# Attention and gated-convolution layer, forward and backward, on one Trainium2 core: the rows of q and of the gradient laid out as four blocks and transposed by one transfer, dP taken out of PSUM by ScalarE, and new leads for the planned order

## The chip, the cores and the metric

The kernel runs on one core of one Trainium2 chip. The core has TensorE (PE; its weight loads are shown as PEld), VectorE (DVE), ScalarE (ACT), GpSimd (POOL) and SyncE (SP), which here does nothing but issue transfers. All engines share SBUF; TensorE writes to PSUM, from which DVE and ACT read. The transfers run on 16 DMA engines.

The metric is the device time in microseconds of one execution. The time before is the median of three runs.

## The reference

`B, T, D, K = 2, 4000, 144, 5`, all in bfloat16. The forward part, cut to what matters:

```
xa  = layernorm(x)
q, k, v = split(xa @ w_qkv)
p   = softmax(q @ k.T * D ** -0.5)
glob = (p @ v) @ w_att_out
u, g = split(gelu(xa @ w_mlp_in))
loc = (u * dwconv(layernorm(g), dw_csgu)) @ w_mlp_out
m   = concat(glob, loc)
out = x + (m + dwconv(m, dw_merge)) @ w_merge
```

The kernel returns `out` and, for a given `grad_out`, the gradients of x and of the seven weights (the `vjp` of this function).

## The kernel before, in words

The 4000 positions of a batch entry are cut into 32 tiles of 125 rows; 64 tiles in all. The attention phase (`phase_att`, L1182) walks them in steps `s`. Weights are multiplied together beforehand, so that scores are a product of a projected row block and the normalised input itself, and the gradient with respect to p, dP, is likewise a product of a projected gradient and that input.

For a tile `i` the following is done, spread over several steps:

- `jit_mm` (L1223): seven matmuls make `pj`, 125 rows x 288: the projected query (144) and the projected gradient (144). ScalarE copies it to `qb` (L1232). POOL copies the last 16 columns of both halves four times each into a second tile `qr` (`rems`, L1240), 32 columns apart, since the matmuls on these 16 columns use four different groups of 32 rows of TensorE.
- `jit_tr` (L1242): TensorE transposes `qb` and `qr` in four blocks of 128 columns (L1246) into a PSUM tile, and ScalarE copies that to `qt` (L1248). `qt` has three buffers.
- `quad` (L1254): in each of the four `products` of a step, two blocks of scores of tile `s` and two blocks of dP of tile `s-1`, 500 columns each, are made from `qt`: four matmuls over 128 rows (L1257) and four over 16 rows (L1264).
- `S_min` (L1279): DVE takes the scores out of PSUM into `Pbuf` with the running minimum; `P_exp` (L1285): ScalarE makes the exponential.
- `PdP` (L1291): dP times P goes to `Sbuf`. In three of the four products ScalarE copies dP out of PSUM (L1295) and DVE multiplies in SBUF (L1297); in the fourth (`q == 3`) DVE multiplies straight from PSUM (L1293).
- SP transposes `Pbuf` to `PT` (L1289) and `Sbuf` to `ST` (L1473), each in two halves of 16 blocks of 128 x 128, by the DMA. `PT` and `ST` have one buffer: a half may be written only after the matmuls on it of the tile before.
- `Y_half` (L1306) and `Z_half` (L1344): 16 matmuls on each half of PT and of ST, into `yz`. From Y come `yn`, which SP stores to Yn_d (L1320), and on POOL the scaled rows `QBs` (L1324 to L1328). From Z comes `zn`, which SP stores (L1349) and transposes to `zt` (L1356).
- `X_group` (L1391): for up to three blocks of 125 rows, matmuls on Sbuf and Pbuf of two tiles, and where they are due on `zt` and `dhT`, into a PSUM tile `X`, which DVE adds to `acc` (L1397).

Between these stand the units of the gated convolution (`local_units`, L577 to L745), which use TensorE, ACT, DVE and POOL, store `ug` and transpose `dhr` to `dhT` on SP's queue (L703); in the second part of the first batch entry the loading and preparation of the second one take their place (SP's loads into gq, xa_aug and others); and at the end the merge and the final weight gradients.

The order of the instructions on each engine from step 2 on is not the program's. The class `Planner` (L779) collects the instructions, groups matmuls, takes what depends on what, gives each group a cost, and lays them out as a list scheduler; each engine then runs its groups in that fixed order. A group's rank is its place in the program plus a lead from the table `LEAD` (L782), whose keys are kind by kind: phase (A or T), engine, tile, size, and for some tiles the turn within a step. A negative lead lets a kind be taken earlier, a positive one later. Steps 0 and 1 (`head`, with `jit_q` L1410 and `jit_b` L1424 for the first two tiles) keep the order of the program. In what depends on what, two readers of one PSUM bank are kept in order only when they are on the same engine (L1012).

Of the kernel before, what the change touches and what calls it, by code (L numbers as in the profile page):

```python
# [8 lines left out]
BF = mybir.dt.bfloat16  # L9
F32 = mybir.dt.float32  # L10
ACT = mybir.ActivationFunctionType
# [767 lines left out]
class Planner:  # L779


    LEAD = {  # L782
# [15 lines left out]
    }  # L798


# [114 lines left out]
    def plan(self, i0, i1, window=400, late=1 << 40):  # L915
# [38 lines left out]
        for ins in todo:  # L954
# [3 lines left out]
            for w, lst in ((False, ins.ins), (True, ins.outs)):  # L958
                for a in lst:
# [42 lines left out]
                    if w:  # L1002
                        for h, q in Rd:
                            if h != g and self.meet(q, bank):
                                preds[g].add(h)
                        full = lambda q: not psum and q[0] >= r[0] and q[1] <= r[1] and len(r[2]) == 1 and q[2][0][0] >= r[2][0][0] and q[2][-1][1] <= r[2][0][1]
                        W[:] = [z for z in W if not full(z[1])]
                        Rd[:] = [z for z in Rd if not full(z[1])]
                        W.append((g, r))
                    else:  # L1010
                        if psum:
                            after[g].update(h for h, _ in Rd if h != g and groups[h]["e"] == groups[g]["e"])  # L1012
                        Rd.append((g, r))
        lastpe = {}
        for g, G in enumerate(groups):
# [166 lines left out]
def phase_att(k, W, SS, A, head, E0, E1, prep, hooks):  # L1182
# [21 lines left out]
    PT = ab.tile([128, NB, 128], BF, name="PT")  # L1204
    ST = ab.tile([128, NB, 128], BF, name="ST")
    QBs = ab.tile([PB, NPB, 2, D], BF, name="QBs")
    qbr = [ab.tile([PB, 2, D], BF, name="qb%d" % i) for i in range(3)]
    qrr = [ab.tile([PB, 256], BF, name="qr%d" % i) for i in range(3)]
    znr = [ab.tile([128, 256], BF, name="zn%d" % i) for i in range(2)]

    def clr():
        for t_ in qrr:
            nc.gpsimd.memset(t_[:], 0.0)
        for t_ in znr:
            nc.gpsimd.memset(t_[:], 0.0)
# [7 lines left out]
    def jit_mm(i):  # L1223
        S, ti = bs(i)
        pj = ps_w.tile([PB, 2 * D], F32, tag="w")
        nc.tensor.matmul(pj[:], S.R[:, ti], W.RW[:, 0:2 * D], start=True, stop=False)
        nc.tensor.matmul(pj[:, 0:D], S.xaT_m[:, ti], W.Q0[:], start=False, stop=False)
        for kk in range(5):
            h = i % NB + 4 - kk
            nc.tensor.matmul(pj[:, D:2 * D], S.goT[:, h * PB:(h + 1) * PB], W.VUT[:, kk, 0:D], start=False, stop=(kk == 4))  # L1230
        qb = qbr[i % 3]
        nc.scalar.copy(qb[:], pj[:].rearrange("p (a b) -> p a b", b=D))  # L1232
        QB[i] = qb
        for h in range(2):
            rems(nc.gpsimd.tensor_copy, i, h)

    def rems(eng, i, h):
        v = qrr[i % 3][:].rearrange("p (a r c) -> p a r c", a=4, r=2)
        v = v[:, 0:4:3, :, 0:DR] if h == 0 else v[:, 1:3, :, 0:DR]
        eng(v, QB[i][:, h, 128:D].rearrange("p (a r c) -> p a r c", a=1, r=1).to_broadcast([PB, 2, 2, DR]))  # L1240

    def jit_tr(i):  # L1242
        qb = QB[i]
        pt = ps_w.tile([128, 4, 128], BF, tag="w")
        for q, src in enumerate((qb[:, 0, 0:128], qrr[i % 3][:, 0:128], qrr[i % 3][:, 128:256], qb[:, 1, 0:128])):
            nc.tensor.transpose(pt[:, q, 0:PB], src, W.ident[0:PB, 0:PB])  # L1246
        qt = gw.tile([128, 4, PB], BF, tag="qt")
        nc.scalar.copy(qt[:], pt[:, :, 0:PB])  # L1248
        QT[i] = qt

    def pchunk(pb, c2):
        return Pbuf[0:PB, pb, c2 * 1024:(c2 + 1) * 1024]
# [1 line left out]
    def quad(work, stacked=True):  # L1254
        pp = [ps_sg.tile([PB, 2, 512], F32, tag="sg", name="ps") for _ in range(len(work) // 2)]
        for r, (i, h, c) in enumerate(work):
            mm = nc.tensor.matmul(pp[r // 2][:, r % 2, 0:CH], QT[i][:, 3 * h, :], bs(i)[0].xaT_m[:, c * CH:(c + 1) * CH], start=True, stop=False)  # L1257
        with tc.issue_after(mm.ins):
            for r, (i, h, c) in enumerate(work):
                S = bs(i)[0]  # L1260
                q = c % 4 if stacked else 3
                rs = slice(32 * q, 32 * q + DR)
                xr = S.XR[rs, (c // 4) * CH:(c // 4 + 1) * CH] if stacked else S.R[rs, c * CH:(c + 1) * CH]
                nc.tensor.matmul(pp[r // 2][:, r % 2, 0:CH], QT[i][rs, 1 + (q // 2 + h) % 2, :], xr, start=False, stop=True)  # L1264
        return [p[:, :, 0:CH].rearrange("p h (a b) -> p h a b", b=PB) for p in pp]

    def S_work(i, c2):
# [142 lines left out]
    def jit_q(i):  # L1410
        S, ti = bs(i)
        pj = ps_w.tile([PB, 2 * D], F32, tag="w")
        nc.tensor.matmul(pj[:, 0:D], S.R[:, ti], W.RW[:, 0:D], start=True, stop=False)
        nc.tensor.matmul(pj[:, 0:D], S.xaT_m[:, ti], W.Q0[:], start=False, stop=True)
        QB[i] = qbr[i % 3]
        nc.scalar.copy(QB[i][:, 0, :], pj[:, 0:D])
        rems(nc.scalar.copy, i, 0)
        QT[i] = gw.tile([128, 4, PB], BF, tag="qt", name="qt")
        pt = ps_w.tile([128, 4, 128], BF, tag="w")
        for q, src in enumerate((QB[i][:, 0, 0:128], qrr[i % 3][:, 0:128], qrr[i % 3][:, 128:256])):  # L1420
            nc.tensor.transpose(pt[:, q, 0:PB], src, W.ident[0:PB, 0:PB])
        nc.scalar.copy(QT[i][:, 0:3, :], pt[:, 0:3, 0:PB])

    def jit_b(i):  # L1424
        S, ti = bs(i)
        pj = ps_w.tile([PB, 2 * D], F32, tag="w")
        nc.tensor.matmul(pj[:, D:2 * D], S.R[:, ti], W.RW[:, D:2 * D], start=True, stop=False)
        for kk in range(5):
            h = i + 4 - kk
            nc.tensor.matmul(pj[:, D:2 * D], S.goT[:, h * PB:(h + 1) * PB], W.VUT[:, kk, 0:D], start=False, stop=(kk == 4))  # L1430
        nc.scalar.copy(QB[i][:, 1, :], pj[:, D:2 * D])
        rems(nc.scalar.copy, i, 1)
        pt = ps_w.tile([128, 4, 128], BF, tag="w")
        for q, src in enumerate((qrr[i % 3][:, 0:128], qrr[i % 3][:, 128:256], QB[i][:, 1, 0:128])):
            nc.tensor.transpose(pt[:, q, 0:PB], src, W.ident[0:PB, 0:PB])
        nc.scalar.copy(QT[i][64:112, 1, :], pt[64:112, 0, 0:PB])
        nc.scalar.copy(QT[i][0:48, 2, :], pt[0:48, 1, 0:PB])
        nc.scalar.copy(QT[i][:, 3, :], pt[:, 2, 0:PB])

    steps = head(dict(pads=pads, clr=clr, jit_q=jit_q, jit_b=jit_b, jit=lambda i: (jit_mm(i), jit_tr(i))))  # L1440
    i0 = 0
# [2 lines left out]
    for s in range(NT + 1):  # L1444
# [30 lines left out]
        def products(q):  # L1475
# [5 lines left out]
            ps = quad(S_work(s, q) + (dP_work(s - 1, q ^ 1) if ok(s - 1) else []))  # L1481
            S_min(s, q, ps[0])
            if ok(s - 1):
                PdP(s - 1, q ^ 1, ps[1], q == 3)

        if s < 2:
            for q in range(8):
# [740 lines left out]
```

## Time and profile before

| | |
|---|---|
| median of 3 runs | 1297.62 us (1297.03 to 1298.73) |
| the profiled execution, its own time | 1296.92 us |
| its span, first to last instruction | 1295.1 us |
| granted TensorE clock, mean | 0.995 |
| matmuls | 15,874 |
| bytes moved by DMA | 185.78 MB, 143 GB/s over the span |

The span in 40 equal slices, where each digit is the busy share in tenths (9 is 90% or more), shows the same picture from some 60 us to 1150 us: TensorE at 9, DVE at 8 to 9, the DMA engines at 6 to 9. Before lies the head (loads, layer norm, products of weights), behind it the merge and the end.

In rows of instructions, "x62 | 35.9, 580 | 30.8 <-PE pt" reads: 62 instructions, 35.9 us busy in all, 580 ns mean duration of one, 30.8 us idle time of that engine just before them, most of it ended by PE writing pt. Matmuls overlap, so the mean duration of one is longer than the distance of two starts. In a list of waits the numbers are the total in us, how many, and the longest. In rows of a single line of the program, "1167/1175/2007" are the least, the median and the greatest duration in ns.

### The profile page before, as it was taken

The numbers are of one execution on the slowest core, as the hardware profiler recorded it, in microseconds if no ns is written. First come the engines' busy times: TensorE is split into PE (matmuls) and PEld (weight loads), VectorE is DVE, ScalarE is ACT, GpSimd is POOL, SyncE is SP. The second block draws the span as 40 slices with busy tenths as digits, with TensorE's granted clock in tenths as the row PEclk, the third lists the DMA queues.
The fourth block names the chain that finished last, engine by engine and source line by source line (L and its number), as shares of the span: only waits on it lengthen the run. The fifth ranks groups of instructions, "written<-read, shape, count | busy, mean of one in ns | idle before, by whom it ended". The sixth has DMA issues, their size and how long they took to land.

```text
span 1295.1 us, 39335 instructions
## 1 busy us (share of the span) xinstructions
PE 1250.1 (97%) x15874; PEld 1034.1 (80%) x15874; DVE 1051.8 (81%) x2808; ACT 787.5 (61%) x1291; POOL 515.2 (40%) x1018
## 2 busy tenths in 40 slices
PE   5899999999999999999899999999999999999998
PEld 3677778888888877777678888888888887799987
DVE  7488888989889887988879888889889887758915
ACT  4766666665666665555666656666665665526561
POOL 7564343443444423332434434343444423142310
PEclk9899999999999999999999999999999999999999
DMA  3488888888886879888898877888778899959602
GB/s 110 88 138 147 140 142 145 145 140 146 153 153 132 153 129 167 167 148 146 176 163 148 146 138 129 155 143 145 149 134 144 129 161 167 187 118 233 200 24 59
DMA packets 628899, 185.78 MB, mean 143 GB/s; under 512 B 604270, under 2 KB 623120, under 8 KB 628696
## 3 DMA queue, kind: packets, MB, share of 16 engines
q1 hardware_dynamic: 627000, 181.67, 76.1%
q8 instruction: 124, 2.03, 0.6%
q0 software_dynamic: 1168, 1.39, 0.4%
q14 instruction: 59, 0.48, 0.1%
q10 hardware_dynamic: 548, 0.21, 0.1%
HBM read 22.96 MB, written 16.69 MB: 31 GB/s over the span
## 4 chain that ended last, share of the span: by engine, by line
PE 82%; DMA 6%; DVE 4%; ACT 3%; POOL 2%; issue 1%; SPq 1%; ACTq 0%; POOLq 0%
PE X L1391 20%; PE ps L1257 14%; PE yz L1344 9%; PE yz L1306 9%; PE ps L1264 6%; PE po L1764 3%; PE Hps L1679 3%; DMA PT<-Pbuf 3%; DVE Pbuf L1279 2%; PE pd L682 1%; PE pc L667 1%; PE pd L615 1%; ACT Pbuf L1285 1%; PE pj L1230 1%; DMA ST<-Sbuf 1%
## 5 line engine op out<-in xcount | busy, mean ns | idle before, releaser
L1279 DVE TENSOR_SCALAR_CACHE_REDUCE Pbuf<-ps 125x1000 bf16<-125x1000 f32 x256 | 306.4, 1197 | 81.9 <-PE ps L1264 79.5
L1285 ACT ACTIVATE Pbuf<-Pbuf,nm 125x1000 bf16<-125x1000 bf16 x256 | 281.8, 1132 | 86.6 <-DVE nm L1281 84.6
L1391 PE MATMUL X<-QBs,Sbuf 125*125 125x144 bf16 x2048 | 297.6, 229 | 0.9 <-DVE acc L1397 0.5
L1391 PE MATMUL X<-QBs,Pbuf 125*125 125x144 bf16 x2048 | 291.9, 226 | 0.6 <-POOL QBs L1328 0.6
L1391 PEld LDWEIGHTS <-Sbuf 125*125 125x125 bf16 x2048 | 259.5, 137 | 24.7 <-issue 24.5
L1257 PE MATMUL ps<-xaT_m,qt 128*125 128x500 bf16 x1024 | 264.7, 378 | 3.1 <-DVE Pbuf L1279 2.4
L1391 PEld LDWEIGHTS <-Pbuf 125*125 125x125 bf16 x2048 | 260.7, 137 | 1.2 <-issue 1.1
L1295 ACT CAST Sbuf<-ps 125x1000 bf16<-125x1000 f32 x190 | 188.9, 994 | 114.5 <-PE ps L1264 111.8
L1397 DVE TENSOR_TENSOR acc<-X,acc 125x432 f32<-125x432 f32 (+1 forms) x373 | 201.0, 549 | 32.3 <-PE X L1391 29.0
L1306 PE MATMUL yz<-xa_aug,PT 125*125 125x145 bf16 x2048 | 148.6, 229 | 10.8 <-DMA PT<-Pbuf 10.5
L1257 PEld LDWEIGHTS <-qt 128*125 128x125 bf16 x1024 | 122.5, 137 | 45.1 <-issue 6.3
L1344 PE MATMUL yz<-xa_aug,ST 125*125 125x144 bf16 x2048 | 150.5, 228 | 6.8 <-DMA ST<-Sbuf 3.9
L1306 PEld LDWEIGHTS <-PT 125*125 125x125 bf16 x2048 | 139.3, 138 | 15.2 <-DMA PT<-Pbuf 12.5
L1344 PEld LDWEIGHTS <-ST 125*125 125x125 bf16 x2048 | 139.6, 138 | 10.4 <-DMA ST<-Sbuf 5.3
L1297 DVE TENSOR_TENSOR Sbuf<-Sbuf,Pbuf 125x1024 bf16<-125x1024 bf16 x190 | 135.5, 716 | 10.4 <-ACT Sbuf L1295 10.2
L1264 PEld LDWEIGHTS <-qt 16*125 16x125 bf16 x1024 | 36.6, 128 | 98.6 <-issue 98.2
L1264 PE MATMUL ps<-XR,qt 16*125 16x500 bf16 x1016 | 111.5, 421 | 0.0
L1326 POOL TENSOR_SCALAR g<-qb,rl 125x144 f32<-125x144 bf16 x64 | 28.3, 442 | 172.1 <-DVE rl L1312 137.2
L1293 DVE TENSOR_TENSOR Sbuf<-ps,Pbuf 125x1000 bf16<-125x1000 f32 x66 | 78.8, 1194 | 3.3 <-issue 1.9
L710 POOL TENSOR_TENSOR A_dwc<-l_fl,A_dwc 128x512 f32<-128x512 f32 (+2 forms) x48 | 37.6, 782 | 88.6 <-ACT l_fl L709 88.5
L585 POOL TENSOR_SCALAR l_a<-l_sq 125x576 bf16<-125x576 bf16 x32 | 22.2, 694 | 108.3 <-ACT l_sq L583 102.0
L1240 POOL COPY qr<-qb 125x64 bf16<-125x64 bf16 x124 | 33.9, 302 | 65.8 <-ACT qb L1232 65.4
(578 smaller groups left out, 2417.9 us busy)
## 6 DMA issues: line engine op xcount, KB each, us to landing
Yn_d<-yn SPq DMA_DIRECT2D x64, 35.2 KB
Zn_d<-zn SPq DMA_DIRECT2D x64, 35.2 KB
ug_d<-ugr SPq DMA_DIRECT2D x32, 70.3 KB
PT<-Pbuf SPq DMA_TRANSPOSE x126
ST<-Sbuf SPq DMA_TRANSPOSE x126
go_h<-in_grad_out_dram SPq DMA_DIRECT2D x8, 252.0 KB
Yg<-Yn_d SPq DMA_DIRECT2D x8, 252.0 KB
Yg<-ug_d SPq DMA_DIRECT2D x8, 252.0 KB
```

The lines of the kernel that those rows point to most:

```text
L1257: mm = nc.tensor.matmul(pp[r // 2][:, r % 2, 0:CH], QT[i][:, 3 * h, :], bs(i)[0].xaT_m[:, c * CH:(c + 1) * CH], start=True, stop=False)
L1264: nc.tensor.matmul(pp[r // 2][:, r % 2, 0:CH], QT[i][rs, 1 + (q // 2 + h) % 2, :], xr, start=False, stop=True)
L1279: nc.vector.tensor_scalar(pv(Pbuf, i % NPB, c2), src, -1.0, 3.0e38, op0=ALU.mult, op1=ALU.min, accum_out=NM[i][:, c2:c2 + 1])
L1285: nc.scalar.activation(v, v, ACT.Exp, bias=NM[i][:, 4:5], scale=-1.0)
L1293: nc.vector.tensor_tensor(pv(Sbuf, i % NDB, c2), src, pv(Pbuf, i % NPB, c2), op=ALU.mult)
L1295: nc.scalar.copy(pv(Sbuf, i % NDB, c2), src)
L1297: nc.vector.tensor_tensor(sc, sc, pchunk(i % NPB, c2), op=ALU.mult)
L1306: nc.tensor.matmul(Y, PT[0:PB, j, 0:PB], S.xa_aug[:, j, 0:D + 1], start=(j == 0), stop=(j == NB - 1))
L1344: nc.tensor.matmul(Z, ST[0:PB, j, 0:PB], S.xa_aug[:, j, 0:D], start=(j == 0), stop=(j == NB - 1))
L1391: nc.tensor.matmul(X[:, jj, :], l, r, start=(n_ == 0), stop=(n_ == len(ops) - 1))
L1397: nc.vector.tensor_tensor(av, X[:, 0:nj, :], av, op=ALU.add)
L1679: nc.tensor.matmul(H[0:rows, a // 3, (a % 3) * D:(a % 3 + 1) * D], lhs, self.src[b][h][:, 2 + j, :], start=(n == 0 and a % 3 == 0), stop=( ...
```

## The change

Four parts.

1. `qb` becomes one tile of 128 x 512 in four blocks of 128 columns: query 0 to 127, query's last 16 columns four times, gradient 0 to 127, gradient's last 16 columns four times. ScalarE's copy of `pj` writes 144 columns each to blocks 0 and 2, so that the first copy of the 16 columns is in place; POOL copies it three times more. `qr` is gone. The three tiles are cleared once at the start.
2. `jit_tr` is one transfer on SP's queue, `qb` to `qt`, in place of four TensorE transposes and ScalarE's copy. In the head TensorE still transposes, two blocks at a time instead of three.
3. `PdP` in the planned steps always goes by ScalarE's copy and DVE's product in SBUF; only the last step and the head still have the direct form.
4. The table `LEAD` is new throughout, with other keys; and two readers of one PSUM bank on different engines are now a true dependency for the planner, of the later one on the earlier one.

```diff
     LEAD = {
-        "A ACT Pbuf 1000 0": 197, "A PE ps 0 0": -160, "A DVE Pbuf 1000 0": 25, "A ACT Sbuf 1000 0": -41, "A DVE Sbuf 1024 0": 198, "A PE ph 0": 39,
+        "A ACT Pbuf 1000 0": 80, "A PE ps 0 0": -215, "A DVE Pbuf 1000 0": 18, "A ACT Sbuf 1000 0": 70, "A DVE Sbuf 1024 0": 60, "A SP PT 2048 0": -96,
...
+        "A DVE rsr 2": 33, "A PE ps 0 1": 36, "A DVE Pbuf 1000 2": -26, "A DVE Sbuf 1024 2": 33, "A SP qt 512": -58, "A PE X 0 2": 38,
...
                         if psum:
-                            after[g].update(h for h, _ in Rd if h != g and groups[h]["e"] == groups[g]["e"])
+                            for h, _ in Rd:
+                                if h != g:
+                                    (after if groups[h]["e"] == groups[g]["e"] else preds)[g].add(h)
...
-    qbr = [ab.tile([PB, 2, D], BF, name="qb%d" % i) for i in range(3)]
-    qrr = [ab.tile([PB, 256], BF, name="qr%d" % i) for i in range(3)]
+    qbr = [ab.tile([128, 512], BF, name="qb%d" % i) for i in range(3)]
...
-        qb = qbr[i % 3]
-        nc.scalar.copy(qb[:], pj[:].rearrange("p (a b) -> p a b", b=D))
-        QB[i] = qb
+        QB[i] = qbr[i % 3][0:PB].rearrange("p (a b) -> p a b", a=2)[:, :, 0:D]
+        nc.scalar.copy(QB[i], pj[:].rearrange("p (a b) -> p a b", b=D))
...
     def rems(eng, i, h):
-        v = qrr[i % 3][:].rearrange("p (a r c) -> p a r c", a=4, r=2)
-        v = v[:, 0:4:3, :, 0:DR] if h == 0 else v[:, 1:3, :, 0:DR]
-        eng(v, QB[i][:, h, 128:D].rearrange("p (a r c) -> p a r c", a=1, r=1).to_broadcast([PB, 2, 2, DR]))
+        v = qbr[i % 3][0:PB].rearrange("p (a c) -> p a c", c=32)
+        eng(v[:, 8 * h + 5:8 * h + 8, 0:DR], v[:, 8 * h + 4:8 * h + 5, 0:DR].to_broadcast([PB, 3, DR]))
 
     def jit_tr(i):
-        qb = QB[i]
-        pt = ps_w.tile([128, 4, 128], BF, tag="w")
-        for q, src in enumerate((qb[:, 0, 0:128], qrr[i % 3][:, 0:128], qrr[i % 3][:, 128:256], qb[:, 1, 0:128])):
-            nc.tensor.transpose(pt[:, q, 0:PB], src, W.ident[0:PB, 0:PB])
-        qt = gw.tile([128, 4, PB], BF, tag="qt")
-        nc.scalar.copy(qt[:], pt[:, :, 0:PB])
-        QT[i] = qt
+        QT[i] = gw.tile([128, 4, 128], BF, tag="qt", name="qt")
+        nc.sync.dma_start_transpose(out=QT[i][:], in_=qbr[i % 3][:])
...
-                nc.tensor.matmul(pp[r // 2][:, r % 2, 0:CH], QT[i][rs, 1 + (q // 2 + h) % 2, :], xr, start=False, stop=True)
+                nc.tensor.matmul(pp[r // 2][:, r % 2, 0:CH], QT[i][rs, 2 * h + 1, 0:PB], xr, start=False, stop=True)
...
-                PdP(s - 1, q ^ 1, ps[1], q == 3)
+                PdP(s - 1, q ^ 1, ps[1], False)
```

More of the change, by code (lines that the diff above doesn't have):

```diff
@@ L1206, in phase_att @@
     QBs = ab.tile([PB, NPB, 2, D], BF, name="QBs")
-    qbr = [ab.tile([PB, 2, D], BF, name="qb%d" % i) for i in range(3)]
-    qrr = [ab.tile([PB, 256], BF, name="qr%d" % i) for i in range(3)]
+    qbr = [ab.tile([128, 512], BF, name="qb%d" % i) for i in range(3)]
     znr = [ab.tile([128, 256], BF, name="zn%d" % i) for i in range(2)]
     def clr():
-        for t_ in qrr:
+        for t_ in qbr:
             nc.gpsimd.memset(t_[:], 0.0)
@@ L1256, in quad @@
         for r, (i, h, c) in enumerate(work):
-            mm = nc.tensor.matmul(pp[r // 2][:, r % 2, 0:CH], QT[i][:, 3 * h, :], bs(i)[0].xaT_m[:, c * CH:(c + 1) * CH], start=True, stop=False)
+            mm = nc.tensor.matmul(pp[r // 2][:, r % 2, 0:CH], QT[i][:, 2 * h, 0:PB], bs(i)[0].xaT_m[:, c * CH:(c + 1) * CH], start=True, stop=False)
         with tc.issue_after(mm.ins):
@@ L1414, in jit_q @@
         nc.tensor.matmul(pj[:, 0:D], S.xaT_m[:, ti], W.Q0[:], start=False, stop=True)
-        QB[i] = qbr[i % 3]
+        QB[i] = qbr[i % 3][0:PB].rearrange("p (a b) -> p a b", a=2)[:, :, 0:D]
         nc.scalar.copy(QB[i][:, 0, :], pj[:, 0:D])
         rems(nc.scalar.copy, i, 0)
-        QT[i] = gw.tile([128, 4, PB], BF, tag="qt", name="qt")
+        QT[i] = gw.tile([128, 4, 128], BF, tag="qt", name="qt")
         pt = ps_w.tile([128, 4, 128], BF, tag="w")
-        for q, src in enumerate((QB[i][:, 0, 0:128], qrr[i % 3][:, 0:128], qrr[i % 3][:, 128:256])):
-            nc.tensor.transpose(pt[:, q, 0:PB], src, W.ident[0:PB, 0:PB])
-        nc.scalar.copy(QT[i][:, 0:3, :], pt[:, 0:3, 0:PB])
+        for q in range(2):
+            nc.tensor.transpose(pt[:, q, 0:PB], qbr[i % 3][0:PB, q * 128:(q + 1) * 128], W.ident[0:PB, 0:PB])
+        nc.scalar.copy(QT[i][:, 0:2, 0:PB], pt[:, 0:2, 0:PB])
     def jit_b(i):
@@ L1433, in jit_b @@
         pt = ps_w.tile([128, 4, 128], BF, tag="w")
[L1434 to L1438, printed above, removed]
+        for q in range(2, 4):
+            nc.tensor.transpose(pt[:, q, 0:PB], qbr[i % 3][0:PB, q * 128:(q + 1) * 128], W.ident[0:PB, 0:PB])
+        nc.scalar.copy(QT[i][:, 2:4, 0:PB], pt[:, 2:4, 0:PB])
     steps = head(dict(pads=pads, clr=clr, jit_q=jit_q, jit_b=jit_b, jit=lambda i: (jit_mm(i), jit_tr(i))))
```

27 rows, old and new, of the table LEAD are left out of this document.

## The prediction

> **What bounds the kernel now.** I read the busy times first, then the chain that ended last, then the busy times by stretch, and last the rows in order of time around one tile's transposes.
>
> ```profile
> PE 1250.1 (97%) x15874; PEld 1034.1 (80%) x15874; DVE 1051.8 (81%) x2808; ACT 787.5 (61%) x1291; POOL 515.2 (40%) x1018
> ...
> PE 82%; DMA 6%; DVE 4%; ACT 3%; POOL 2%; issue 1%; SPq 1%; ACTq 0%; POOLq 0%
> ```
>
> TensorE is busy nearly throughout and is 82% of the chain. The average hides stages, so the stretches (columns: window, length, busy time and count by engine, granted clock, DMA share, GB/s):
>
> ```profile
> 60.00:240.00 180.00, 174.82 (x2118) 140.05 (x2118) 153.77 (x389) 118.72 (x196) 86.11 (x173) 0.99 0.82 141
> 240.00:500.00 260.00, 259.32 (x3315) 213.60 (x3314) 224.59 (x578) 166.62 (x270) 107.89 (x205) 1.00 0.83 145
> 500.00:640.00 140.00, 130.36 (x1603) 104.14 (x1601) 119.19 (x300) 80.28 (x110) 46.30 (x99) 1.00 0.84 161
> 640.00:680.00 40.00, 37.00 (x455) 29.89 (x451) 32.74 (x81) 26.54 (x45) 18.24 (x37) 1.00 1.00 165
> 680.00:1100.00 420.00, 419.31 (x5335) 344.61 (x5336) 362.89 (x923) 268.07 (x422) 173.34 (x331) 1.00 0.83 145
> 1100.00:1150.00 50.00, 47.04 (x628) 40.08 (x627) 33.70 (x69) 23.74 (x32) 10.37 (x23) 1.00 0.81 167
> ```
>
> In 240 to 500 and 680 to 1100 us, 680 us together, TensorE is idle for 0.7 us each time: whatever is taken from it there shortens the run. The other four stretches hold 5.2 + 9.6 + 3.0 + 3.0 = 20.8 us of idle time. The waits of TensorE from 60 to 1150 us say what for:
>
> ```profile
> PE yz L1306 <- DMA PT<-Pbuf: 7.9, 7, 2.1
> PE yz L1344 <- DMA ST<-Sbuf: 3.9, 4, 1.5
> ```
>
> The largest are transposes that land late. A tile (17.4 us: 23 half transposes into PT in 200 us) asks the one DMA queue for two halves of PT, two of ST, one zt and half a dhT.
>
> **What the change removes from TensorE.** The four transposes of a tile, in order of time:
>
> ```profile
> 315.26 0.43 PE L1264 MATMUL ps<-XR,qt 16*125 16x500 bf16 x4
> 315.62 0.23 PE L1246 MATMUL pt<-ident,qb 125*128 125x125 bf16 x1
> 315.69 0.27 PE L1246 MATMUL pt<-ident,qr 125*128 125x125 bf16 x2
> 315.80 0.22 PE L1246 MATMUL pt<-ident,qb 125*128 125x125 bf16 x1
> 315.86 0.23 PE L1391 MATMUL X<-QBs,Sbuf 125*125 125x144 bf16 x1
> ```
>
> A single one is shown as 0.22 us, but they overlap: the first starts at 315.62, the next matmul at 315.86. So the price is 0.24 us a tile, and 62 x 0.24 = 14.9 us. Of the 62 tiles 39 lie in the two full stretches (680 / 17.4), worth 9.4 us that nothing else covers; 23 lie where a wait may swallow it, 5.5 us. In the head four further transposes go: 0.2 us. I take all 15.1 us and book new waits apart. (The Trainium skill's page Perfetto Trace Analysis, Identifying the Most-Contended Engine, calls matmul busy time a poor measure of headroom and points to weight loads, which are at 80% here. By that a fifth of TensorE would be spare and the removal worth nothing; the gapless starts at 0.06 us speak against it.)
>
> **What it adds.** One transpose of 128x512 a tile on SP's queue. No row shows that size; the neighbours are two blocks (zt), six (dhT) and sixteen (PT):
>
> ```profile
> L1356 SPq DMA_TRANSPOSE zt<-zn x62: 1167/1175/2007, 72.7 to 1141.3; - x62
> L703 SPq DMA_TRANSPOSE dhT<-dhr x32: 1209/1239/2077, 138.0 to 1076.4; - x32
> L1289 SPq DMA_TRANSPOSE PT<-Pbuf x126: 1536/2242/3999, 41.2 to 1128.6; - x126
> ...
> q1 hardware_dynamic: 627000, 181.67, 76.1%
> ```
>
> Four blocks lie between zt and dhT: 1.2 us on SP, and from issue to the last packet between their medians of 1.7 and 2.3 us; I take 2.0. On the engines: the packet records hold 556,549 packets of 256 bytes, 128 to a block, whose time comes to 829.6 us of sixteen engines, 0.191 us a block. So 0.76 us a tile, 47 us in all, and the DMA share of a stretch rises by some 0.045, from 0.83 to about 0.88.
>
> The Trainium skill speaks against this step: VectorE: DVE Perf Modes, Rules for kernel authors, prefers TensorE for a 128x128 transpose and the DMA only where PSUM is no good destination; its table gives 390 ns against 1309 ns. By these, as an estimate, a tile would give up 1.6 us of TensorE and ask 5.2 us of DMA; the rows say 0.24 and 0.76, both smaller for being pipelined, in the same direction.
>
> Is qt in time? The chain is ACT qb (0.41 us), two POOL copies (0.30 each), SP and landing (2.0): 3.3 us. In the built order the end of a tile's pj and the first matmul with its qt lie 7.5 to 14.3 us of TensorE work apart, so 4 us and more stay for queueing, except in the first planned tile, where it is 4.0: I book 0.5 us there, bounds 0 and 2.
>
> What waits behind it? SP issues in order. In the built order the second half of PT mostly stands right behind qt, and qt waits for POOL's copies, whose pj ends 3.5 to 5 us after the Y matmuls that set PT free. So PT's second half, then ST, Zn_d and zt, go out later. In 240 to 440 us the last packet of a PT half now lands 6.8 us (median) before its first matmul, least 3.1; ST 6.6, least 2.5: that covers it. In 440 to 640 us the medians are 4.5 and 4.7 and the least 0.5. There each late transpose is a TensorE wait. Bounds: 0, and the 23 tiles of the pressed stretches paying all of their 0.76 us, 17.5. Between, I take the ten tiles of 500 to 680 us paying half: 10 x 0.38 = 3.8 us.
>
> **What lies beside the path.** The rows:
>
> ```profile
> L1295 ACT CAST Sbuf<-ps 125x1000 bf16<-125x1000 f32 x190 | 188.9, 994 | 114.5 <-PE ps L1264 111.8 <-DMA PT<-Pbuf 1.7
> L1297 DVE TENSOR_TENSOR Sbuf<-Sbuf,Pbuf 125x1024 bf16<-125x1024 bf16 x190 | 135.5, 716 | 10.4 <-ACT Sbuf L1295 10.2
> L1293 DVE TENSOR_TENSOR Sbuf<-ps,Pbuf 125x1000 bf16<-125x1000 f32 x66 | 78.8, 1194 | 3.3 <-issue 1.9 <-ACT Pbuf L1285 0.7 <-PE ps L1264 0.7
> L1248 ACT COPY qt<-pt 128x500 bf16<-128x500 bf16 x62 | 35.9, 580 | 30.8 <-PE pt L1246 30.2
> ```
>
> 62 of the 66 direct products become a copy by ScalarE and a product in bf16: DVE 62 x (716 - 1194) = -29.6 us, ACT 62 x (994 - 580) = +25.7 us with the copy of qt gone. ACT goes from 61% to 63%, DVE from 81% to 79%. The last quarter of dP is done 994 + 716 - 1194 = 516 ns later, under the 6.6 us that ST lands early; uncovered it would be 32 us. DVE's relief could take at most the 2.4 us that TensorE waits for L1279. I book 0. POOL copies 48 numbers for 64, and clears three tiles of twice the width (310 ns each now, some 0.9 us more, ahead of a POOL wait of 2.13 us): 0.
>
> The new leads reorder everything. Bounds: the 20.8 us of idle time could go, or come once more; I take 0.
>
> **The sum.** -15.1 + 3.8 + 0.5 = -10.8 us on the profiled execution's 1296.9 (span 1295.1 and 1.8 around it): 1286.1. The median of the runs shown is 0.7 higher, so 1287.
>
> **Rivals.** (a) SP becomes the bound: slower. Its rows, semaphore events included, cover 86% of 240 to 440 us: 15.0 of 17.4 us a tile, and 16.2 with the new issue, against 17.16 that TensorE needs. If the wait for POOL's copies leaves x us a tile that SP cannot catch up, the cycle is 16.2 + x: TensorE starts waiting at x = 0.96, the kernel is slower from x = 1.2, and x = 1.35 gives 62 x 0.15 = 9 us, some 1307. For it: the 3.5 to 5 us by which qt's data come after PT's. Against: SP runs 6 us ahead now, and part of its waits vanish once it is late. (b) The DMA engines give it all back: the pressed tiles pay 17.5 instead of 3.8 us, 1287 + 14 = 1301; at 13 it is no change, 1297. For it: shares up to 1.00 in 640 to 680 us. Against: the full stretches keep 9.4 us in either case. (c) The new order also clears half of the 20.8 us: 1287 - 10 = 1277. For it: these waits hang on when a transpose is issued, which is what the leads set; against: more transposes for the same queue. That the change does not do what it says can be left out: the built program has 252 fewer matmuls and 62 more transposes on SP.
>
> **How the numbers follow.** The forecast 0.60 (its own range 1280 to 1294), (a) 0.15, (b) 0.13, (c) 0.12. The range of 1276 to 1304 leaves out the far part of (a) and the best of (c), under 0.2. About 0.2% (2.6 us) is what a measurement can tell from no change. Faster: 0.60 + 0.12 + 0.03 of (b) = 0.75; same: 0.08 of (b); slower: 0.15 + 0.02 = 0.17.
>
> **What would show it.** Right: no transposes of qb left on TensorE, its busy time about 15 us lower, still idle under 2 us in the two full stretches; DMA share near 0.88; SP's qt issues near 1.2 us. TensorE's waits for PT and ST a few us higher, between 500 and 680 us. Wrong: waits of TensorE for qt in many tiles, or for PT and ST in the full stretches (then (a)); or waits that shrink (then (c)).

## The result, and the profile after

The changed kernel takes 1303.1 us (median of 9 runs, 1299.17 to 1306.87), the kernel before 1297.62 us (9 runs): a ratio of 1.0034 with a 95% interval of 1.0019 to 1.0049. By the ratio it is slower by 4.4 us (2.5 to 6.4); 11 us faster was forecast. The profiled execution took 1303.26 us, its span is 1301.5 us.

The busy times and the chain, from the page of the changed kernel:

```profile
PE 1245.2 (96%) x15622; PEld 1026.9 (79%) x15622; DVE 1022.3 (79%) x2808; ACT 814.6 (63%) x1287; POOL 529.4 (41%) x1018
...
PE 80%; DMA 9%; ACT 3%; DVE 3%; POOL 2%; SPq 2%; issue 1%; ACTq 0%; DVEq 0%; POOLq 0%
```

The 252 matmuls are gone, but TensorE's busy time fell by 4.9 us and not by 15.1; DMA's share of the chain rose from 6% to 9%. The stretches of the changed kernel (columns as before: window, length, busy time and count by engine, granted clock, DMA share, GB/s):

```profile
60.00:240.00 180.00, 173.71 (x2117) 139.86 (x2116) 152.43 (x401) 121.98 (x194) 92.35 (x173) 0.99 0.88 150
240.00:500.00 260.00, 259.89 (x3301) 213.84 (x3297) 218.48 (x581) 175.08 (x269) 115.25 (x211) 1.00 0.91 155
500.00:640.00 140.00, 126.01 (x1455) 98.19 (x1455) 109.41 (x285) 81.30 (x103) 43.18 (x87) 0.95 0.92 160
640.00:680.00 40.00, 35.38 (x416) 28.86 (x415) 29.71 (x78) 23.17 (x39) 18.63 (x34) 0.96 0.93 159
680.00:1100.00 420.00, 419.00 (x5299) 343.63 (x5298) 354.31 (x931) 281.58 (x429) 175.55 (x337) 1.00 0.87 153
1100.00:1150.00 50.00, 43.39 (x533) 35.69 (x531) 30.27 (x60) 23.19 (x27) 6.47 (x13) 0.97 0.89 175
```

In the two full stretches TensorE is as full as before (idle 0.1 and 1.0 us). Where the time is won and lost can be read from the ends of the Y matmuls of each tile, though the two orders differ and single tiles stray by some us. From tile 14 to tile 24 they end 5.3 to 7.8 us earlier than in the kernel before (tile 24: 478.0 us for 485.9). From 500 to 680 us TensorE is idle for 18.6 us instead of 12.6, and in these stretches and from 1100 us on the granted clock is no longer 1.00. By tile 28 the lead is gone (554.2 us for 554.3), and at tile 38 the changed kernel is 4.1 us behind. The second full stretch wins that back (tile 58: 1066.9 for 1067.4). From tile 61 (1117.2 in both) to tile 63 (1151.7 for 1147.3) another 4.4 us are lost.

TensorE's longest waits for transposes from 60 to 1150 us, where the kernel before had 7.9 us for PT and 3.9 for ST:

```profile
PE yz L1338 <- DMA ST<-Sbuf: 8.1, 8, 3.0
PE yz L1300 <- DMA PT<-Pbuf: 5.6, 8, 1.2
PE ps L1251 <- DMA qt<-qb: 4.3, 2, 3.7
```

One of these places, in order of time, TensorE and then SP's queue of the changed kernel (start, duration, line, what, and in brackets the idle time and what ended it):

```profile
544.13 1.18 PE L1338 MATMUL yz<-xa_aug,ST 125*125 125x144 bf16 x16
549.00 1.85 PE L1251 MATMUL ps<-xaT_m,qt 128*125 128x500 bf16 x4 [3.69 <-DMA qt<-qb]
550.78 0.68 PE L1258 MATMUL ps<-XR,qt 16*125 16x500 bf16 x4
```

```profile
537.57 3.73 SPq L1465 DMA_TRANSPOSE ST<-Sbuf  x1
541.39 0.43 SPq L1314 DMA_DIRECT2D Yn_d<-yn  x1
541.88 0.32 SPq L43 DMA_DIRECT2D gq<-in_grad_out_dram  x1
542.29 1.85 SPq L1283 DMA_TRANSPOSE PT<-Pbuf  x1
544.20 1.01 SPq L43 DMA_DIRECT2D gq<-in_grad_out_dram  x1
545.26 1.17 SPq L1350 DMA_TRANSPOSE zt<-zn  x1
546.54 1.20 SPq L1243 DMA_TRANSPOSE qt<-qb  x1
```

POOL had finished the copies for this qt at 538.97. SP came to it at 546.54, having issued one thing after the other without a pause worth the name, and its last packet was written at 548.49. TensorE stood from 545.31 to 549.00. What follows is slow too: the four matmuls of 500 columns take 1.85 us, where the same four took 1.01 us in the kernel before. The clock that TensorE was granted says why. It is at one half from 549.1 to 552.5 us. After the first 60 us and before the last microseconds this happens once in the kernel before (3.4 us) and six times in the changed one (3.4, 3.4, 3.4, 6.8, 3.4 and 3.4 us), near the end of a wait of 2.1 to 3.7 us or, the last, of 1.9. The one in the kernel before comes just after a wait of 1.4 us.

The Trainium skill's page TensorE: Matmul & The Clock Gate, HAM oscillation, gives the rule as no idle gap of more than some 3.4 us. That the clock halves after a wait is as the trace shows it; the length is not, since 2.09 us (at 99.28) were followed by a half clock here, and 1.43 us (at 77.43) in the kernel before, while 2.07 us (at 631.28) in the kernel before were not. The measurement decides.

With this the account of the two profiled executions closes. TensorE's busy time should fall by 15.1; after the first 60 us it was busy for 22.1 us at half clock instead of 3.4, half of which is lost: (22.1 - 3.4) / 2 = 9.4. That makes 1250.1 - 15.1 + 9.4 = 1244.4, and 1245.2 were measured. Idle time rose from 45.1 to 56.3 us. Busy -4.9 and idle +11.2 are the +6.4 of the span.

### The profile page after: what moved, and what is told of

The parts are those of the page before. It is cut to its first block, busy times and chain, and to the rows that moved or that the text cites. A ratio compares the mean times of both kernels' runs of the same rounds, so it can differ in the third digit from the quotient of the medians.

```text
span 1301.5 us, 38976 instructions
## 1 busy us (share of the span) xinstructions
PE 1245.2 (96%) x15622; PEld 1026.9 (79%) x15622; DVE 1022.3 (79%) x2808; ACT 814.6 (63%) x1287; POOL 529.4 (41%) x1018
## 4 chain that ended last, share of the span: by engine, by line
PE 80%; DMA 9%; ACT 3%; DVE 3%; POOL 2%; SPq 2%; issue 1%; ACTq 0%; DVEq 0%; POOLq 0%
PE X L1385 20%; PE ps L1251 15%; PE yz L1300 9%; PE yz L1338 9%; PE ps L1258 6%; DMA ST<-Sbuf 3%; PE po L1756 2%; PE Hps L1671 2%; DMA PT<-Pbuf 2%; PE pd L682 1%; PE pc L667 1%; PE pd L615 1%; PE pj L1231 1%; PE pw L727 1%; PE pw L742 1%
## 5 line engine op out<-in xcount | busy, mean ns | idle before, releaser
L1289 ACT CAST Sbuf<-ps 125x1000 bf16<-125x1000 f32 x252 | 250.6, 994 | 257.1 <-PE ps L1258 250.7
L1273 DVE TENSOR_SCALAR_CACHE_REDUCE Pbuf<-ps 125x1000 bf16<-125x1000 f32 x256 | 306.1, 1196 | 93.5 <-PE ps L1258 91.5
L1291 DVE TENSOR_TENSOR Sbuf<-Sbuf,Pbuf 125x1024 bf16<-125x1024 bf16 x252 | 175.7, 698 | 8.9 <-ACT Sbuf L1289 8.9
L1300 PE MATMUL yz<-xa_aug,PT 125*125 125x145 bf16 x2048 | 151.6, 230 | 7.3 <-DMA PT<-Pbuf 7.1
L1300 PEld LDWEIGHTS <-PT 125*125 125x125 bf16 x2048 | 140.0, 138 | 17.3 <-DMA PT<-Pbuf 10.0
L1320 POOL TENSOR_SCALAR g<-qb,rl 125x144 f32<-125x144 bf16 x64 | 31.6, 493 | 171.9 <-DVE rl L1306 141.3
L1239 POOL COPY qb<-qb 125x48 bf16<-125x48 bf16 x124 | 36.7, 325 | 61.8 <-ACT qb L1233 61.1
L1671 PE MATMUL Hps<-Yg,go_h 125*128 125x144 bf16 x640 | 53.4, 229 | 1.9 <-DMA Yg<-ug_d 1.9
```

Source lines behind the costliest of these rows:

```text
L1273: nc.vector.tensor_scalar(pv(Pbuf, i % NPB, c2), src, -1.0, 3.0e38, op0=ALU.mult, op1=ALU.min, accum_out=NM[i][:, c2:c2 + 1])
L1289: nc.scalar.copy(pv(Sbuf, i % NDB, c2), src)
L1291: nc.vector.tensor_tensor(sc, sc, pchunk(i % NPB, c2), op=ALU.mult)
L1300: nc.tensor.matmul(Y, PT[0:PB, j, 0:PB], S.xa_aug[:, j, 0:D + 1], start=(j == 0), stop=(j == NB - 1))
L1671: nc.tensor.matmul(H[0:rows, a // 3, (a % 3) * D:(a % 3 + 1) * D], lhs, self.src[b][h][:, 2 + j, :], start=(n == 0 and a % 3 == 0), stop=( ...
```

## The experiments

Twelve kernels. In those that let the planner lay out a new order, the order is part of the difference; where it says that the order was kept, the sequence of instructions on each engine is the same but for what is named. A ratio is against runs of the kernel before taken beside the experiment, whose medians lay between 1298.8 and 1299.7 us, so differences of a few us are to be taken from the ratios.

**Old leads.** The changed kernel with the table `LEAD` of before.

```diff
-        "A ACT Pbuf 1000 0": 80, "A PE ps 0 0": -215, "A DVE Pbuf 1000 0": 18,
+        "A ACT Pbuf 1000 0": 197, "A PE ps 0 0": -160, "A DVE Pbuf 1000 0": 25,
...
```

> The changed kernel with the table of leads of the kernel before; all else as changed. Load theory (the added transpose, 0.76 us of the DMA engines and 1.24 us of SP a tile, makes TensorE wait where the queue is pressed, and waits of 2 us and more halve its clock for 3.4 us): the load is the same, so 1299 to 1308, with some 18 us of TensorE idle from 500 to 680 us and four or more stretches at half clock. Order theory (the new leads make the waits, whatever is transferred): the old leads give the forecast gain, 1284 to 1290, and at most two stretches at half clock.

Measured: 1341.1 us, ratio 1.0322 (1.0308 to 1.0336). Both theories missed: the old table costs the new structure 38 us. TensorE is idle for 87.2 us, 22.6 of them in the stretches that were full.

**New leads alone.** The kernel before with the new table and the new dependency.

```diff
-        "A ACT Pbuf 1000 0": 197, "A PE ps 0 0": -160, "A DVE Pbuf 1000 0": 25,
+        "A ACT Pbuf 1000 0": 80, "A PE ps 0 0": -215, "A DVE Pbuf 1000 0": 18,
...
```

> The kernel before with only the new table of leads and the new dependency between readers of a PSUM bank. Load theory: about as before, 1294 to 1301, one or two stretches at half clock, TensorE idle for 500 to 680 us near the 12.6 us of before. Order theory: the 21 us lost by the changed kernel are there without its gain, 1310 to 1318.

Measured: 1313.13 us, 1.0108 (1.0094 to 1.0122). As the order theory has it by number; but the run before shows that a table can do badly on a structure that is not its own, so neither run speaks of the transfer.

**Transposes back on TensorE**, all else as changed.

```diff
-        nc.sync.dma_start_transpose(out=QT[i][:], in_=qbr[i % 3][:])
+        pt = ps_w.tile([128, 4, 128], BF, tag="w")
+        for q in range(4):
+            nc.tensor.transpose(pt[:, q, 0:PB], qbr[i % 3][0:PB, q * 128:(q + 1) * 128], W.ident[0:PB, 0:PB])
+        nc.scalar.copy(QT[i][:, :, 0:PB], pt[:, :, 0:PB])
```

> The changed kernel (four-block layout, new leads, dP by ScalarE) with the four transposes of a tile back on TensorE and the copy of qt back on ScalarE. Load theory: the waits go and 15 us of TensorE come back: 1294 to 1301, at most two stretches at half clock, DMA share in the full stretches near 0.83. Order theory: the waits stay and the 15 us are added: 1313 to 1320.

Measured: 1303.8 us, 1.0039 (1.0026 to 1.0051), where the changed kernel has 1303.1. With 15 us more on TensorE it takes the same time: in this comparison the transfer gives back all that it saves, though the order is a new one here too. Idle from 500 to 680 us is 12.2 us again, the half clock 12.5 us for 22.1. The load theory's number was missed by 3 us, the order theory's by 9.

**dP's last quarter by VectorE again.**

```diff
-                PdP(s - 1, q ^ 1, ps[1], False)
+                PdP(s - 1, q ^ 1, ps[1], q == 3)
```

> The changed kernel with the last quarter of dP again multiplied by VectorE straight from PSUM. Load theory and order theory: no part in it, 1300 to 1307. Third theory (the copy by ScalarE puts off the last quarter of dP by 0.52 us a tile, so ST is late): the waits for ST go, 8 us and the half clock behind them, 1289 to 1295.

Measured: 1311.52 us, 1.0098 (1.0075 to 1.0121), 8 us above the changed kernel. All three theories missed it, the first two by 4.5 us. The time did not fall, so nothing here speaks for the third; how much of the 8 us is the direct form's and how much the new order's cannot be told.

**The load alone, order kept.** The kernel before, with 62 transposes that nobody needs.

```diff
-        nc.sync.dma_start_transpose(out=PT[:, a:a + w, :], in_=Pbuf[:, i % NPB, a * 128:(a + w) * 128])
+        p = nc.sync.dma_start_transpose(out=PT[:, a:a + w, :], in_=Pbuf[:, i % NPB, a * 128:(a + w) * 128])
+        if h == 0 and i > 0:
+            d = nc.sync.dma_start_transpose(out=more[:], in_=W.VUT[:].rearrange("p a b -> p (a b)")[:, 0:512])
+            k.PL.extra.add(d.ins.name)
+            k.PL.behind[p.ins.name] = [d.ins]
```

The planner leaves out what is in `extra` and, once the order stands, puts it behind its neighbour.

> The kernel before, with the order of every engine kept as it was, and 62 more transposes of 128x512 put into SP's queue behind the first half of PT of each tile; they go from a constant weight into a tile that nobody reads. Nothing else is changed, TensorE's four transposes stay. Load theory (the transfer itself is what gives the 15 us back): 8 to 16 us more, 1306 to 1315, TensorE idle from 500 to 680 us some 18 us for 12.6, three or more stretches at half clock for one. Order theory (a transfer more or less is covered, the new order waits by itself): at most 3 us more, 1297 to 1302.

Measured: 1318.21 us, 1.0136 (1.0117 to 1.0155), 17.7 us more by the ratio, somewhat above the 8 to 16 that the load theory gave. No computation changed and nobody waits for these transposes. Its stretches, and TensorE's longest waits from 60 to 1150 us:

```profile
500.00:680.00 180.00, 159.85 (x1923) 128.11 (x1923) 142.02 (x353) 98.78 (x140) 60.65 (x125) 0.98 0.86 158
680.00:1100.00 420.00, 418.25 (x5316) 343.57 (x5315) 364.05 (x927) 270.71 (x428) 174.81 (x333) 1.00 0.91 151
```

```profile
PE yz L1350 <- DMA ST<-Sbuf: 9.7, 8, 2.7
PE yz L1312 <- DMA PT<-Pbuf: 9.7, 10, 1.6
```

The full stretch stays full; 500 to 680 us goes from 12.6 to 20.2 us of idle time, and the two waits from 11.8 to 19.4 us. So a loss of the size in question is there without a new order: the load alone makes it.

**The same on the changed kernel**, order kept: the same edit.

> The changed kernel, order kept, with the same 62 unread transposes beside its own. Load theory: the queue was already short, so 12 to 30 us more, 1315 to 1333, idle also in the stretches that were full. Order theory: at most 3 us more, 1300 to 1306.

Measured: 1363.4 us, 1.0485 (1.0465 to 1.0505). Twice what was expected at most: some 60 us above the changed kernel, where the same 62 transposes cost 18 on the kernel before. The two kernels differ in order and leads as well as in the transposes that SP has already. TensorE is now idle in the full stretches also (14.3 and 15.3 us), and 49.7 us at half clock.

**qt earlier in SP's queue**, order kept on the other engines.

```diff
+        sp = order["SP"]
+        for g in list(sp):
+            if groups[g]["ins"][0].outs[0].bass_ap.tensor.name.startswith("qt"):
+                n = sp.index(g)
+                while n and times[sp[n - 1]] >= ready[g] - 2.0:
+                    sp[n - 1], sp[n] = sp[n], sp[n - 1]
+                    n -= 1
```

> The changed kernel with the order of all engines kept, but SP's: each qt transpose goes ahead of the entries that the plan issues less than 2 us before its data are ready or later. If the place of qt in the queue makes the loss: TensorE's wait for qt (4.3 us, and the half clock behind it) goes, 1294 to 1299. If it is the load as such: what qt gains PT, ST and zt lose, 1300 to 1307.

Measured: 1306.87 us, 1.0058 (1.0043 to 1.0073). TensorE's waits for transposes in this kernel:

```profile
PE yz L1307 <- DMA PT<-Pbuf: 11.8, 10, 2.9
PE yz L1345 <- DMA ST<-Sbuf: 8.9, 7, 2.1
```

The wait for qt fell from 4.3 to 0.3 us and that for zt from 2.7 to 0.3; the one for PT rose from 5.6 to 11.8 us and that for ST from 8.1 to 8.9. What one entry of the queue gains others lose: a better place for qt alone does not bring the time back.

**Split.** The changed kernel with TensorE's transposes for tiles 27 to 38 and 60 to 63.

```diff
+        if 27 <= i <= 38 or i >= 60:
+            pt = ps_w.tile([128, 4, 128], BF, tag="w")
...
+        else:
+            nc.sync.dma_start_transpose(out=QT[i][:], in_=qbr[i % 3][:])
```

> The changed kernel with TensorE's transposes for the tiles made between some 500 and 700 us (27 to 38) and the last ones (60 to 63), and the transfer for the other 46. Load theory: most of 46 x 0.24 = 11 us is kept and the waits from 500 to 680 us fall back to about 12 us: 1291 to 1298. Order theory: no better than the changed kernel, 1301 to 1310.

Measured: 1297.72 us, 0.9987 (0.9972 to 1.0002): 6 us below the changed kernel by the ratios, at the upper edge of what the load theory gave, and level with the kernel before. Idle from 500 to 680 us is 13.4 us.

**Which part of the load.** A transpose takes SP's time to issue and the engines' time to move. Two kernels set them apart, both on the kernel before with the order kept: the unread transpose cut to one block, and in its place a plain transfer of as much engine time.

```diff
-            d = nc.sync.dma_start_transpose(out=more[:], in_=W.VUT[:].rearrange("p a b -> p (a b)")[:, 0:512])
+            d = nc.sync.dma_start_transpose(out=more[:], in_=W.VUT[:].rearrange("p a b -> p (a b)")[:, 0:128])
```

> As the loaded kernel before (order kept, 62 unread transposes behind the first half of PT), but of one block of 128x128 each: SP's issue stays near 1.2 us, the DMA engines' work falls from 0.76 to 0.19 us. If SP's in-order issue is what is short: most of the 18 us stays, 1311 to 1319. If it is the DMA engines: a quarter of it, 1300 to 1305.

Measured: 1315.77 us, 1.0133 (1.0116 to 1.0151).

```diff
-            d = nc.sync.dma_start_transpose(out=more[:], in_=W.VUT[:].rearrange("p a b -> p (a b)")[:, 0:512])
+            d = nc.sync.dma_start(more[:], W.VUT[:].rearrange("p a b -> p (a b)")[:, 0:1152])
```

> As the loaded kernel before, but in place of each unread transpose a plain transfer of 128 rows of 2304 bytes out of SBUF to memory that nobody reads: by the packets of that size (93 ns each) 0.74 us of the DMA engines, as the transpose of four blocks, but some 0.4 us of SP's issue. If SP's issue is short: a third, 1302 to 1307. If it is the DMA engines: most of the 18 us, 1311 to 1319.

Measured: 1309.46 us, 1.0081 (1.0063 to 1.0100): between the two ranges, so neither was met, and the issue took SP twice the 0.4 us supposed. SP's issue time, the row of each of the three (four blocks, one block, plain; least, median and greatest ns):

```profile
L1293 SPq DMA_TRANSPOSE more<-VUT x62: 1193/1450/1912, 54.2 to 1144.9; - x62
```

```profile
L1293 SPq DMA_TRANSPOSE more<-VUT x62: 1132/1461/2098, 54.6 to 1141.5; - x62
```

```profile
L1293 SPq DMA_DIRECT2D more<-VUT x62: 340/798/1405, 54.4 to 1136.6; - x62
```

One block takes SP as long as four, and costs the kernel as much (ratios 1.0133 and 1.0136) with a quarter of the bytes. The plain transfer takes SP 0.80 us (median) and costs 10.5 us. In sums of SP's time from 60 to 1150 us, 91, 90 and 50 us cost 17.7, 17.3 and 10.5 us, by the ratios: 0.19 to 0.21 for one. The time of all packets, spread over the sixteen engines, rose by 75.9, 18.4 and 71.0 us over the kernel before. So four blocks and one block ask the same of SP and cost the same, while four blocks and the plain transfer ask the same of the engines and cost 17.7 and 10.5 us. With one block the DMA share from 500 to 680 us is no higher than before (0.84 and 1.00 in its two parts then), and TensorE waits and slows all the same:

```profile
500.00:680.00 180.00, 163.05 (x1934) 131.34 (x1932) 143.46 (x360) 97.63 (x138) 61.17 (x126) 0.96 0.82 153
```

The loss goes with SP's time to issue, in order, and not with the engines' time to move. Two things stay open. No run issues the transposes from another engine, so SP's own time and that of its queue are not told apart. And the price of an issue is not fixed: with the plain transfers SP's other entries took 19 us longer, so that SP's rows from 60 to 1150 us rose by 93, 89 and 69 us in all.

**SP relieved.** ScalarE issues the 64 stores of Yn_d, order kept, in the changed kernel and in the split one.

```diff
-        nc.sync.dma_start(S.Yn_d[:, j0, :], yn[:])
+        d = nc.scalar.dma_start(S.Yn_d[:, j0, :], yn[:])
...
+            k.PL.moved.add(d.ins.name)
+            k.PL.behind[t_.ins.name] = [d.ins]
```

> The changed kernel, order of all engines kept, with the 64 stores of Yn_d issued by ScalarE behind its own two copies of that tile instead of by SP. SP theory (what is short is SP's time to issue, in order): SP is relieved of some 0.59 us a tile, 36 us in all, which at the price found with the unread transposes (17.5 us for 90 us of issue, 0.19) is 7 us: 1294 to 1299. If the bytes are what is short: nothing, 1301 to 1306. If ScalarE's own 0.4 us a tile count: slower, 1306 to 1312.

Measured: 1298.18 us, 0.9997 (0.9981 to 1.0012) to the kernel before: 5 us below the changed kernel by the ratios, with the same bytes, in the range of the SP theory. The store takes 0.26 us of its new issuer's time (median) where it took 0.65 of SP's. But SP was not relieved of 36 us: the stores had taken 41.5 us from 60 to 1150 us, and SP's rows fell by 12.7 us only (968.3 to 955.6), above all since the transposes into PT and ST took some 23 us longer to issue. The price of 0.19 is not confirmed by this run. The store's wait for its data left SP's order too. The rows of the store, in the changed kernel and in this one:

```profile
L1314 SPq DMA_DIRECT2D Yn_d<-yn x64: 250/650/1227, 64.5 to 1153.7; - x64
```

```profile
L1315 ACTq DMA_DIRECT2D Yn_d<-yn x64: 256/257/282, 63.7 to 1149.0; - x64
```

The Trainium skill's page DMA: Bandwidth & Descriptors, Rules for kernel authors, says that spreading transfers over issuing engines brings no bandwidth and saves only the sequencer's issue time. This run agrees in that time was gained with the same bytes moved.

> The split kernel (transfer for 46 tiles, TensorE for the tiles of the pressed stretch and the last four) with the same stores issued by ScalarE, order kept. SP theory: 3 to 7 us below the split kernel, 1290 to 1295, ahead of both kernels. Bytes: as the split kernel, 1296 to 1300.

Measured: 1296.32 us, 0.9982 (0.9963 to 1.0000). The fastest of all by its median, but its interval just reaches the kernel before; that it beats both kernels is shown against the changed one only. The SP theory missed here: 3 to 7 us below the split kernel were expected, and it is under 1 us by the ratios, in the range given for the bytes (the intervals leave room for some 3 us). So moving the stores is shown to help only where all 62 transposes are on SP's queue.

## Why the prediction was wrong

**TensorE's 15.1 us: right.** The matmuls went, and the busy time, with the half clock taken out, fell by as much to within 0.8 us. In the split kernel, where 46 tiles have the transfer, the same account gives 1250.1 - 46 x 0.24 - 0.2 + (13.3 - 3.4) / 2 = 1243.8, measured 1243.7.

**"Between, I take the ten tiles of 500 to 680 us paying half: 10 x 0.38 = 3.8 us": the step that failed.** It priced the new transfer by the DMA engines' 0.76 us. The price hangs on SP's 1.2 us or more of issue, as the one-block transpose shows, and for 62 of them it is 17.7 us (15.2 to 20.1) at the order of before, by itself more than the 15.1 saved. The upper bound of that term, 17.5 us, was the size of it, for a different reason. Rival (b), which took this bound and ended at 1301, came nearest to the time by luck: it charged the DMA engines. That 1303.1 lies just inside the widest range, 1276 to 1304, is no merit of the working either: the range reached so far for the rivals' sake, and the forecast was of a faster kernel.

**What was not in the sum: the clock.** A late transpose can cost its wait and then 3.4 us, in the changed kernel once 6.8, of TensorE at half speed. This is 9.4 of the 20.6 us given back in the profiled pair (the rest is the 11.2 us of idle time). It is read off the trace and the account; no run held the clock up during a wait, so it was not shown by itself.

**The cover of 6.8 and 6.6 us between landing and first use** was right for the full stretches, where it shrank to 3.5 and 3.8 us (medians, 240 to 440 us; the least are 0.8 and 0.6) and TensorE hardly waited. It was no cover where SP also issues the loads of the second batch entry and the spills of acc: SP's rows cover 91.5% of 500 to 680 us in the kernel before and 93.8% after. I had read SP's share in 240 to 440 us alone. The share by itself does not tell the stretches apart, though: in 240 to 440 us it rose from 86% to 93.1%, and TensorE did not wait there. That the further loads make the difference is read off SP's rows; no run took them away.

**Rival (a)** named the resource, SP, and ended at 1307. Its form was wrong: it had every tile pay. The full stretches do not pay at all (idle 0.1 and 1.0 us); some twenty tiles pay for all.

**Booked at nothing:** VectorE fell by 29.5 us and ScalarE rose by 27.1, as forecast (29.6 and 25.7), and with VectorE's direct form the changed kernel is 8 us slower, so there is no sign that this part is a loss. The leads at 0 were a guess: with the old table the changed structure takes 38 us more. -15.1 + 17.7 is +2.6 us, and 4.4 were measured; the other 2 us are within the interval of the 17.7, or lie between dP, the leads and the places in the queue, and the runs, which plan anew with each of these, cannot part them.

Two figures of the working were off without bearing on the outcome: 0.41 + 2 x 0.30 + 2.0 is 3.0 us and not 3.3, and the 47 us asked of the DMA engines came to 66 (the time of all packets, over sixteen engines).

Of the marks named ahead, the two full stretches, the share of the DMA engines (0.87 to 0.93) and the 1.2 us to issue qt came as said, and the waits were looked for in the right place. They were too few and too cheap in the sum. TensorE's busy time, named as about 15 us lower, fell by 4.9, with the half clock in it.

## What to carry to other kernels

A transfer that takes work off a full engine was paid here in the issuing queue's time, which for a small transpose did not shrink with its bytes: add up that time by stretch before the change, and beside it how long before its first use each transfer lands. The cheapest test is to put the new transfers, unread, into the old kernel with its order kept; here that one run showed the outcome. And a wait on TensorE is to be priced with the half clock behind it.

## What the runs showed of the hardware that was not expected

- Transposes of one, two and four blocks of 128x128 take SP nearly the same time: 1.13, 1.17 and 1.19 us at the least. A plain store took a median of 0.65 us on SP's crowded queue and 0.26 us from ScalarE.
- In the kernel before and the changed one, waits of 1.4 to 3.7 us came with 3.4 us at half clock (one of 2.7 us with 6.8), and three of 1.5 to 2.1 us without. The account of busy times by halves holds to 1.4 us in nine kernels: the changed and the split one, the two with SP relieved, those with the transposes back on TensorE and with qt early, and the three loads on the kernel before. It falls short by 2.2 us with the new leads alone, 3.8 with the direct form, 6.9 with the old leads and 7.5 in the changed kernel with the load.
- The price of the load is not the same everywhere: 62 unread transposes cost 17.7 us on the kernel before and some 60 us on the changed one, which has 62 of its own and another order.
